# Transposing q and k on the way in instead of on TensorE, and making scores two batches ahead, in a fused sliding-window attention and GEGLU kernel

## The chip, the cores and the metric

The kernel runs on one core of a Trainium2 chip. The metric is the time of one execution in device microseconds. TensorE (PE in the profile) multiplies, VectorE (DVE) and ScalarE (ACT) do elementwise work, GpSimd (POOL) and SyncE (SP) only issue DMAs here.

## The reference

Attention over 8 batches, 8 heads, 576 positions, 64 channels per head, followed by a gated feed-forward layer on the 4608 resulting rows of 512:

```
scores = q @ k^T / 8
mask, heads 0..3 ("plain"):   0 <= i - j < 32
mask, heads 4..7 ("dilated"): 0 <= i - j < 128 and (i - j) % 4 == 0
attn = softmax(where(mask, scores, -1e9));  x = attn @ v      # per head
out  = (gelu(x @ w_gate) * (x @ w_val)) @ w_out               # 512 -> 1536 -> 512
```

A plain query sees at most 32 keys before it. A dilated query sees only keys of its own class (its position modulo 4), at most 32 of them, so each class of 144 positions is a plain window of its own.

## The kernel before

The work has two kinds. The unit of the attention is a "row tile" n: one batch and one pair of heads, so four per batch (two plain pairs, two dilated) and 32 in all. The unit of the feed-forward layer is a chunk c of 512 output rows, nine in all. A batch has 576 rows, so chunk c needs batches c and, but for its first rows, nothing later than c+1.

A row tile passes these steps. `t_q` and `t_k` transpose q and k on TensorE into PSUM (L152 and L170, `t_mm`), 18 transposes in all, the four classes of a 512-position block one by one and the 64 remaining positions apart; `copy` brings them to SBUF (ACT at L184, DVE at L186). `emit_s` makes the scores of four key blocks and a tail block with ten matmuls (L228) in PSUM banks 4 to 7, exponentiates them on ACT (L234, L235) and multiplies with a 0/1 mask on DVE (L236). `emit_pv` multiplies with v and with ones, for the row sums (L297). `norm_r` (L302 to L306) turns the sums into reciprocals along the free dimension on DVE and `norm_x` (L317 plain, L320 dilated) multiplies and writes the transposed result xT, which is FFN1's input. No maximum is subtracted.

A chunk has FFN1, 12 steps of 8 matmuls (L332) with gelu on ACT (L336) and the product on DVE (L337), and FFN2, four blocks of 12 matmuls (L341), each followed by a copy to SBUF (`osb`, L354 on DVE) and a store that SP issues (L356). Each matmul moves 512 columns.

Instructions run in program order on each engine; the schedule is written out by hand in the loop over chunks. A prologue makes all of batch 0. In chunk c the row tiles of `t_list` are transposed between FFN1's steps, those of `pv_list` get their PV and normalisation between FFN1's steps, and the scores of `s_list` are made between FFN2's blocks. When a score's batch is needed by the very next chunk (`now_pv`, chunks 0 and 1), PV and normalisation stand between FFN2's blocks as well, and FFN2 then uses one PSUM bank for all four blocks:

```
bank = 0 if now_pv else tb
ffn2(c, tb, bank)
do_s()
do_pv()
store(c, tb, bank)
```

Loads are issued by POOL in program order, fp32 in DRAM to fp16 in SBUF: q, k of batch 0, v of batch 0, gate and value weights, q, k of batch 1, output weights, v of batch 1, then in chunk c q, k and v of batch c+2. A q or k load (L117) has rows of four positions, 1 KB in DRAM; the plain half of v (L130) has rows of one position, 256 B.

Of the kernel before, what the change touches and what calls it, by code (L numbers as in the profile page):

```python
# [14 lines left out]
WIN = 32  # L15
# [24 lines left out]
def kernel(  # L40
# [22 lines left out]
    scale = 1.0 / np.sqrt(D)  # L63

# [10 lines left out]
    vpl = ctx.enter_context(tc.tile_pool(name="vpl", bufs=4))  # L75
    qtp = ctx.enter_context(tc.tile_pool(name="qtp", bufs=8))
# [18 lines left out]
    u_t = [const.tile([P, CH], F16, tag=f"u{i}", name=f"u{i}") for i in range(NNB)]  # L95

# [14 lines left out]
    tiles = {}  # L111
    def load_qk(b):
        qm = ldp.tile([P, H, 4, D], F16, tag="qm", name=f"qm{b}")
        km = ldp.tile([P, H, 4, D], F16, tag="km", name=f"km{b}")
        rem = ldp.tile([P, H, D], F16, tag="rem", name=f"rem{b}")
        for t, src in ((qm, q), (km, k)):
            nc.gpsimd.dma_start(  # L117
                out=t.rearrange("p h r d -> p h (r d)"),
                in_=src[b, :, 0 : 4 * P, :].rearrange("h (p r) d -> p h (r d)", r=4),
            )  # L120
        nc.gpsimd.dma_start(out=rem[0:64], in_=q[b, :, 4 * P : S, :].rearrange("h p d -> p h d"))
        nc.gpsimd.dma_start(out=rem[64:128], in_=k[b, :, 4 * P : S, :].rearrange("h p d -> p h d"))
        tiles["qk", b] = (qm, km, rem)

    def load_v(b):
        vp = vpl.tile([P, 4, 4, D], F16, tag="vp", name=f"vp{b}")
        vd = vpl.tile([P, 4, 4, D], F16, tag="vd", name=f"vd{b}")
        vt = vpl.tile([P, H, D], F16, tag="vt", name=f"vt{b}")
        for kb in range(4):
            nc.gpsimd.dma_start(  # L130
                out=vp[:, kb, :, :],
                in_=v[b, 0:4, kb * P : (kb + 1) * P, :].rearrange("h p d -> p h d"),
            )
        nc.gpsimd.dma_start(out=vt, in_=v[b, :, S - P : S, :].rearrange("h p d -> p h d"))
# [9 lines left out]

    def t_q(n, bank, eng_main, eng_rem):
        b, hp = divmod(n, NHP)
        qm, km, rem = tiles["qk", b]
        qk = qtp.tile([P, 2, S], F16, tag="qkT", name=f"qkT{n}")
        tiles["qkT", n] = qk
        t_mm(qm, hp, bank)  # L150
        for hl in range(2):
            nc.tensor.transpose(  # L152
                ps16[64 * hl : 64 * hl + 64, bank, 512:640], rem[:, 2 * hp + hl, :], ident
            )
        t_main(n, 0, bank, eng_main)
        src = ps16[:, bank, 512:640]
        if is_plain(n):
            copy(eng_rem, qk[:, :, 4 * P : S], src.rearrange("p (t u) -> p t u", t=2))
        else:
            copy(  # L160
                eng_rem,
                qk[:, 0, :].rearrange("p (r i) -> p r i", r=4)[:, :, P:NCL],
                src[:, 0:64].rearrange("p (i r) -> p r i", r=4),
            )
            copy(eng_rem, qk[:, 1, 4 * P : S], src[:, 64:128])

    def t_mm(src, hp, bank):
        for r in range(4):
            for hl in range(2):
                nc.tensor.transpose(  # L170
                    ps16[64 * hl : 64 * hl + 64, bank, r * P : (r + 1) * P],
                    src[:, 2 * hp + hl, r, :],
                    ident,
                )

    def t_k(n, bank, eng_main):
        b, hp = divmod(n, NHP)
        qm, km, rem = tiles["qk", b]
        t_mm(km, hp, bank)
        t_main(n, 1, bank, eng_main)  # L180
# [300 lines left out]
```

## Time and profile before

| | us |
|---|---|
| time, median of 3 runs (lowest to highest) | 450.51 (448.86 to 451.04) |
| the profiled execution | 451.33 |
| its span, first to last instruction | 449.5 |
| PE busy | 369.9 (82%) |
| DVE busy | 218.5 (49%) |
| ACT busy | 184.0 (41%) |
| POOL busy (issuing DMAs) | 69.1 (15%) |

Busy shares are averages over stages that differ, so they don't say what a stage waits for; the busy time by stage and the chain of waits do. Matmuls overlap, so the duration of one is longer than the step from one to the next. The granted clock of TensorE is given as a share of full speed.

### The profile page before, as it was taken

The page shows a single profiled execution, that of the slowest core. Times are in us where ns is not written, and L with a number is a line of the kernel's source. Part 1 is how long each engine was busy: PE and PEld are TensorE (multiplying, and loading weights), DVE is VectorE, ACT ScalarE, POOL GpSimd, SP SyncE. Part 2 cuts the span into 40 slices and gives each one's busy share as a digit, 9 for nine tenths or more (in the row PEclk, how much of TensorE's full clock was granted, in tenths as well). Part 3 has the DMA queues.
Part 4 walks back from the last instruction along what each step waited for, and adds up shares of the span by engine and source line. Part 5 has one row for each costly group of instructions (what it writes and reads, how often), then busy time and mean ns, then how long its engine had stood idle before and what let it go on. Part 6 is the DMA issues. An engine that isn't in the chain of part 4 may idle for free.

```text
span 449.5 us, 7001 instructions
## 1 busy us (share of the span) xinstructions
PE 369.9 (82%) x2960; PEld 177.7 (40%) x2960; DVE 218.5 (49%) x315; ACT 184.0 (41%) x288; POOL 69.1 (15%) x93
## 2 busy tenths in 40 slices
PE   0637975556777555799999999999999999999996
PEld 0523433222333222345445445544544444444442
DVE  0484314334211534678367656845774793332332
ACT  1531465120666411655647555654655220230320
POOL 6723606000052500000600510000000000000000
PEclk9955999668999988899999999999999999999999
DMA  9999969301069910000930591002001101101002
GB/s 164 181 204 200 180 50 137 53 23 47 1 79 96 155 45 25 25 1 4 149 108 2 73 139 48 1 1 95 0 3 48 48 0 48 47 1 70 23 2 94
DMA packets 64928, 30.03 MB, mean 67 GB/s; under 512 B 34944, under 2 KB 60032, under 8 KB 64896
## 3 DMA queue, kind: packets, MB, share of 16 engines
q0 software_dynamic: 59280, 19.40, 39.4%
q1 hardware_dynamic: 5616, 10.17, 6.0%
q8 instruction: 23, 0.38, 0.3%
q14 instruction: 9, 0.07, 0.0%
HBM read 39.53 MB, written 9.44 MB: 109 GB/s over the span
## 4 chain that ended last, share of the span: by engine, by line
PE 78%; DVE 12%; ACT 6%; DMA 2%; issue 1%; POOL 1%; DVEq 0%; POOLq 0%
PE ps L332 43%; PE ps L341 24%; PE ps L170 5%; PE ps L297 4%; ACT qkT L184 3%; PE ps L228 3%; DVE rb L306 2%; DVE xT L320 2%; DVE dt L302 2%; DMA rem<-in_k_dram 2%; DVE P L236 2%; ACT P L234 1%; DVE osb L354 1%; ACT P L235 1%; DVE xT L317 1%; DVE rc L304 1%
## 5 line engine op out<-in xcount | busy, mean ns | idle before, releaser
L341 PE MATMUL ps<-wo,u 128*128 128x512 f16 x432 | 108.6, 409 | 29.8 <-DVE osb L354 29.8
L337 DVE SCALAR_TENSOR_TENSOR u<-g,ps 128x512 f16<-128x512 f16 x108 | 74.3, 688 | 113.4 <-PE ps L332 106.1
L332 PE MATMUL ps<-xT,wg 128*128 128x512 f16 x432 | 114.3, 387 | 5.0 <-DVE xT L320 4.7
L336 ACT ACTIVATE g<-ps 128x512 f16<-128x512 f32 x108 | 65.7, 608 | 127.2 <-PE ps L332 125.0
L332 PE MATMUL ps<-xT,wv 128*128 128x512 f16 x432 | 112.7, 384 | 0.0
L184 ACT COPY qkT<-ps 128x512 f16<-128x512 f16 (+2 forms) x102 | 61.0, 668 | 48.8 <-PE ps L152 28.1
L341 PEld LDWEIGHTS <-u 128*128 128x128 f16 x432 | 43.3, 104 | 85.4 <-issue 43.3
L332 PEld LDWEIGHTS <-wv 128*128 128x128 f16 x432 | 42.8, 99 | 57.7 <-issue 5.6
L234 ACT ACTIVATE P<-ps 128x800 f16<-128x800 f32 (+1 forms) x32 | 25.7, 804 | 74.3 <-PE ps L228 74.2
L332 PEld LDWEIGHTS <-wg 128*128 128x128 f16 x432 | 38.4, 99 | 44.9 <-issue 3.0
L354 DVE TENSOR_SCALAR osb<-ps 128x512 f32<-128x512 f32 x36 | 24.5, 689 | 27.1 <-PE ps L341 27.1
L236 DVE TENSOR_TENSOR P<-P,mask_d 128x1296 f16<-128x1296 f16 x16 | 13.2, 831 | 38.7 <-ACT P L235 38.7
L117 POOL DMA_DIRECT2D qm<-in_q_dram x8 | 7.3, 909 | 154.8 <-PE ps L152 151.6
L236 DVE TENSOR_TENSOR P<-P,mask_p 128x1440 f16<-128x1440 f16 x16 | 14.5, 908 | 27.9 <-ACT P L235 27.9
L302 DVE STREAM_TRANSPOSE dt<-ps 128x576 f32<-128x576 f32 x32 | 25.0, 781 | 3.3 <-PE ps L297 3.3
L170 PE MATMUL ps<-ident,km 128*64 128x128 f16 x256 | 14.0, 232 | 14.4 <-ACT qkT L184 14.4
L306 DVE STREAM_TRANSPOSE rb<-rc 128x576 f32<-128x576 f32 x32 | 24.9, 778 | 1.1
L130 POOL DMA_DIRECT2D vp<-in_v_dram x32 | 24.1, 786 | 6.0 <-DMA km<-in_k_dram 2.0
L320 DVE TENSOR_TENSOR xT<-ps,rb 128x576 f16<-128x576 f32 x16 | 23.0, 1436 | 0.2
L235 ACT ACTIVATE P<-ps 128x640 f16<-128x640 f32 (+1 forms) x32 | 21.5, 672 | 0.0
L170 PE MATMUL ps<-ident,qm 128*64 128x128 f16 x256 | 14.2, 236 | 8.8 <-DMA qm<-in_q_dram 8.8
L228 PE MATMUL ps<-qkT 64*128 64x160 f16 (+3 forms) x320 | 17.2, 234 | 4.5 <-ACT P L234 1.9
(32 smaller groups left out, 194.2 us busy)
## 6 DMA issues: line engine op xcount, KB each, us to landing
out_dram<-osb SPq DMA_DIRECT2D x36, 256.0 KB, 2.0
qm<-in_q_dram POOLq DMA_DIRECT2D x8, 512.0 KB, 6.1
km<-in_k_dram POOLq DMA_DIRECT2D x8, 512.0 KB, 8.3
vp<-in_v_dram POOLq DMA_DIRECT2D x32, 64.0 KB, 6.9
vd<-in_v_dram POOLq DMA_DIRECT2D x8, 256.0 KB, 4.5
wg<-in_moe_w_gate_dram POOLq DMA_DIRECT2D x3, 512.0 KB, 10.7
wv<-in_moe_w_val_dram POOLq DMA_DIRECT2D x3, 512.0 KB, 12.4
wo<-in_moe_w_out_dram POOLq DMA_DIRECT2D x3, 512.0 KB, 16.2
```

Source lines behind the costliest of these rows:

```text
L170: nc.tensor.transpose(ps16[64 * hl : 64 * hl + 64, bank, r * P : (r + 1) * P], src[:, 2 * hp + hl, r, :], ident,)
L184: nc.scalar.copy(dst, src)
L228: nc.tensor.matmul(o, lhs, rhs, start=True, stop=True)
L234: nc.scalar.activation(pvh[:, :, 0:half], sb[:, 0, :, 0:half], AF.Exp, bias=0.0, scale=scale)
L236: nc.vector.tensor_tensor(pv, pv, mask_p if is_plain(n) else mask_d, ALU.mult)
L302: nc.vector.transpose(dt.rearrange("p b c -> p (b c)"), den)
L306: nc.vector.transpose(rb.rearrange("p (b c) -> p b c", c=32), bass.AP(tensor=rc.tensor, offset=rc.offset, ap=[rc.ap[0], [1, 18], [0, 32]]),)
L320: nc.vector.tensor_tensor(dst.rearrange("p (i b s) -> p b s i", b=2, s=2), num, rb.rearrange("p (b s i) -> p b s i", b=2, s=2), ALU.mult,)
L332: nc.tensor.matmul(ps[:, b0 + gi, :], w[:, kc, ns], xT[kc][:, tok], start=(kc == 0), stop=(kc == NKC - 1))
L336: nc.scalar.activation(g, ps[:, b0, :], AF.Gelu)
L337: nc.vector.scalar_tensor_tensor(u_t[nb], g, USCALE, ps[:, b0 + 1, :], ALU.mult, ALU.mult)
L341: nc.tensor.matmul(ps[:, bank, :], u_t[fc][:, tb * P : (tb + 1) * P], wo_t[fc // 4][:, fc % 4, :], start=(fc == 0), stop=(fc == NNB - 1),)
```

## The change

q and k of batches 1 to 7 are no longer transposed on TensorE. POOL loads them as before into SBUF, and SP then issues DMA transposes from SBUF to SBUF (`dma_start_transpose`), seven per batch. The plain heads are loaded in five blocks of 128 positions for that. Batch 0 is still transposed on TensorE, with the plain heads loaded first.

The transposed q and k of batch b are complete before its scores are made, and scores come a batch earlier: chunk 0 makes those of batches 1 and 2 (eight row tiles), chunk c those of batch c+2. Only chunk 0 has PV and normalisation in its tail. The first S of a chunk stands after FFN1's last step, the next ones inside FFN2's blocks: `ffn2` takes the number of the matmul before which they stand, and a function that makes them.

In dilated heads, two neighbouring classes (2m and 2m+1) of one head lie on the two halves of the 128 partitions after a transpose. A dilated row tile has 16 score matmuls (per head and class one of 144 columns and one of 16, the latter for the last 16 positions of a class) in place of ten, and one exponential in place of two. PV has 24 matmuls as before; `norm_x` writes in the order of positions.

The first batch's mask is added in PSUM: before the scores, four matmuls of the identity with a bias tile (0 or -60000, made from the mask on DVE) fill the banks. All other batches keep the multiplication on DVE, with one mask read for both heads or all four blocks. Stores are issued by ACT instead of SP. Buffers of v go from four to three, with a separate buffer for the last 16 positions per class that four memsets fill with zeros once. Output weights are loaded after v of batch 1.

```
     def load_qk(b):
+        qp = ldp.tile([P, 5, 2, HK, D], F16, tag="qp", name=f"qp{b}")
+        qd = ldp.tile([P, 2, HK, 4, D], F16, tag="qd", name=f"qd{b}")
+        rd = ldp.tile([16, 2, HK, 4, D], F16, tag="rd", name=f"rd{b}", bufs=1)
+        for t, src in ((0, q), (1, k)):
+            nc.gpsimd.dma_start(
+                out=qd[:, t].rearrange("p h r d -> p h (r d)"), in_=quads(src, b, HK, 0, 4 * P)
+            )
...
+        for kb in range(5):
+            n = min(P, S - kb * P)
+            for t, src in ((0, q), (1, k)):
+                nc.gpsimd.dma_start(
+                    out=qp[0:n, kb, t],
+                    in_=src[b, 0:HK, kb * P : kb * P + n, :].rearrange("h p d -> p h d"),
+                )
+        qtp_ = qtp.tile([P, 2, 2, S], F16, tag="qTp", name=f"qTp{b}")
+        qtd_ = qtp.tile([P, 2, HK, 2, NCL], F16, tag="qTd", name=f"qTd{b}")
+        tiles["qT", b] = (qtp_, qtd_)
+        dst = qtd_.rearrange("p t h m i -> p (t h m) i")
+        nc.sync.dma_start_transpose(out=dst[:, :, 0:P], in_=qd.rearrange("p t h r d -> p (t h r d)"))
+        nc.sync.dma_start_transpose(out=dst[:, :, P:NCL], in_=rd.rearrange("p t h r d -> p (t h r d)"))
+        dst = qtp_.rearrange("p t h c -> p (t h) c")
+        for kb in range(5):
+            n = min(P, S - kb * P)
+            nc.sync.dma_start_transpose(
+                out=dst[:, :, kb * P : kb * P + n], in_=qp[0:n, kb].rearrange("p t h d -> p (t h d)")
+            )
...
     def emit_s(n, b0, pe_mask=False):
...
+            if pe_mask:
+                for i in range(4):
+                    mm(ps[:, b0 + i, 0:DW], ident, bias_d, start=True, stop=False, skip_group_check=True)
+            for hl in range(2):
+                for m in range(2):
+                    for c0, k0, q0, q1 in ((m * NCL, 0, 0, NCL), (2 * NCL + 16 * m, 16, P, NCL)):
+                        for s in range(2):
+                            kt = qtd_[64 * s : 64 * s + 64, 1, 2 * hp + hl, m, :]
+                            qt = qtd_[64 * s : 64 * s + 64, 0, 2 * hp + hl, m, :]
+                            o = ps[:, b0 + 2 * s + hl, c0 : c0 + q1 - q0]
+                            mm(o, kt[:, k0 : k0 + P], qt[:, q0:q1], start=st, stop=True, skip_group_check=True)
...
     def norm_x(n, b0):
...
-            num = ps[:, b0 : b0 + 2, 0 : 2 * NCL].rearrange("p b (s i) -> p b s i", s=2)
+            num = ps[:, b0 : b0 + 2, 0 : 2 * NCL].rearrange("p s (m i) -> p i m s", m=2)
             nc.vector.tensor_tensor(
-                dst.rearrange("p (i b s) -> p b s i", b=2, s=2),
+                dst.rearrange("p (i m s) -> p i m s", m=2, s=2),
                 num,
-                rb.rearrange("p (b s i) -> p b s i", b=2, s=2),
+                rb.rearrange("p (s m i) -> p i m s", s=2, m=2),
                 ALU.mult,
             )
...
-        nc.sync.dma_start(out=out[t0 : t0 + P, :], in_=osb)
+        nc.scalar.dma_start(out=out[t0 : t0 + P, :], in_=osb)
...
     for c in range(NCH):
...
+        pv_list = list(range(NHP * (c + 1), NHP * (c + 2))) if 1 <= c < B - 1 else []
+        if c == 0:
+            s_list = list(range(NHP, 3 * NHP))
+        elif c + 2 < B:
+            s_list = list(range(NHP * (c + 2), NHP * (c + 3)))
+        else:
+            s_list = []
...
+            if nb == NNB - 1 and (c == 0 or c + 2 < B):
+                emit_s(emit_s_pe, SB)
...
+        if c == 0:
+            ffn2(c, 0, 0)
+            store(c, 0, 0, "dve")
+            ffn2(c, 1, 0, 3, s_next)
+            store(c, 1, 0, "dve")
+            pv_all(NHP, 1)
+            ffn2(c, 2, 0, 3, s_next)
+            store(c, 2, 0, "act")
+            pv_all(NHP + 1, 1)
+            ffn2(c, 3, 0, 3, s_next)
+            store(c, 3, 0, "act")
+            pv_all(NHP + 2, 1)
+            s_next()
+            pv_all(NHP + 3, 1)
+            while s_list:
+                s_next()
+        else:
+            ffn2(c, 0, 0)
+            store(c, 0, 0, "act")
+            ffn2(c, 1, 1, 5, s_next)
+            store(c, 1, 1, "act")
+            ffn2(c, 2, 2, 0, s_next)
+            ffn2(c, 3, 3, 0, s_next)
+            store(c, 2, 2, "act")
+            store(c, 3, 3, "dve")
```

## Rows read from the trace of the kernel before

**Rows 1.** The page's first line.

```profile
span 449.5 us, 7001 instructions
```

**Rows 2.** Busy time by stage; the first line names the columns.

```profile
core 0: us, PE busy (x) PEld busy (x) DVE busy (x) ACT busy (x) POOL busy (x), PEclk, DMA share, GB/s
0.00:38.93 38.93, 13.66 (x212) 10.48 (x213) 18.77 (x31) 11.45 (x14) 19.79 (x30) 0.80 1.33 184
38.93:70.14 31.21, 26.41 (x167) 11.81 (x168) 7.57 (x11) 15.22 (x27) 12.92 (x17) 0.92 1.14 126
70.14:110.68 40.54, 23.00 (x189) 10.37 (x188) 18.00 (x25) 7.84 (x10) 5.34 (x8) 0.75 0.50 69
110.68:147.86 37.18, 27.59 (x239) 13.28 (x240) 7.57 (x11) 23.07 (x41) 11.43 (x15) 1.00 0.60 62
147.86:188.62 40.76, 22.60 (x225) 11.07 (x226) 18.70 (x27) 11.10 (x16) 4.09 (x6) 0.86 0.43 55
188.62:217.12 28.50, 28.50 (x266) 13.70 (x267) 21.05 (x30) 17.27 (x30) 4.13 (x6) 0.96 0.20 30
229.53:256.80 27.27, 27.27 (x266) 13.30 (x266) 19.56 (x29) 15.02 (x27) 4.12 (x6) 1.00 0.23 42
256.80:269.22 12.42, 12.42 (x90) 5.63 (x90) 5.86 (x8) 7.86 (x10) 3.64 (x5) 1.00 1.25 145
348.61:373.26 24.65, 24.18 (x193) 11.82 (x192) 19.28 (x29) 7.16 (x12) 0.00 (x0) 1.00 0.06 22
383.62:414.70 31.08, 31.08 (x145) 14.07 (x144) 11.02 (x16) 7.16 (x12) 0.00 (x0) 1.00 0.09 34
```

**Rows 3.** Chain of waits, prologue and start of chunk 0: start us, us, what.

```profile
3.80 9.43 DMA rem<-in_k_dram
...
22.48 0.70 DVE dt L302
...
37.44 1.44 DVE xT L320
38.93 15.83 PE ps L332 x61
```

**Rows 4.** TensorE's waits: line, releaser, us in total, times, longest.

```profile
PE ps L341 <- DVE osb L354: 29.8, 6, 5.3
PE ps L170 <- ACT qkT L184: 14.4, 12, 1.5
```

**Rows 5.** Timeline of chunk 0's tail: start us, us, engine, line, operation.

```profile
72.69 0.91 DVE L236 TENSOR_TENSOR P<-P,mask_p 128x1440 f16<-128x1440 f16 x1 [1.75 <-ACT P L235]
...
78.60 0.68 DVE L354 TENSOR_SCALAR osb<-ps 128x512 f32<-128x512 f32 x1
...
79.34 5.28 PE L341 MATMUL ps<-wo,u 128*128 128x512 f16 x12 [4.85 <-DVE osb L354]
```

**Rows 6.** DMA queues (packets, MB, share); issues (count, KB, us to landing).

```profile
q0 software_dynamic: 59280, 19.40, 39.4%
q1 hardware_dynamic: 5616, 10.17, 6.0%
...
out_dram<-osb SPq DMA_DIRECT2D x36, 256.0 KB, 2.0
...
ident<-attn_identity SPq DMA_DIRECT2D x1, 32.0 KB, 1.9
```

**Rows 7.** Groups by line and shape: count, busy us, mean ns, idle before.

```profile
L130 POOL DMA_DIRECT2D vp<-in_v_dram x32 | 24.1, 786 | 6.0 <-DMA km<-in_k_dram 2.0 <-DMA qm<-in_q_dram 1.9 <-DMA wv<-in_moe_w_val_dram 1.8
L320 DVE TENSOR_TENSOR xT<-ps,rb 128x576 f16<-128x576 f32 x16 | 23.0, 1436 | 0.2
L236 DVE TENSOR_TENSOR P<-P,mask_p 128x1440 f16<-128x1440 f16 x16 | 14.5, 908 | 27.9 <-ACT P L235 27.9
...
L317 DVE TENSOR_TENSOR xT<-ps,rb 128x576 f16<-128x576 f32 x16 | 12.1, 753 | 0.2
```

**Rows 8.** The store's line: duration ns, min, median, max.

```profile
L356 SPq DMA_DIRECT2D out_dram<-osb x36: 332/332/373, 79.3 to 446.5; - x36
```

More of the change, by code (lines that the diff above doesn't have):

```diff
@@ L63 @@
     scale = 1.0 / np.sqrt(D)
+    PW, PT, DW = 160, 80, 320
+    POFF = [0, PW, 2 * PW + PT, 3 * PW + PT, 2 * PW]
+    PH = 4 * PW + PT
+    PB = 2 * PW + PT
     ctx.enter_context(tc.manual_schedule())
@@ L95 @@
     u_t = [const.tile([P, CH], F16, tag=f"u{i}", name=f"u{i}") for i in range(NNB)]
+    vr_t = [const.tile([P, HK, 4, D], F16, tag=f"vr{i}", name=f"vr{i}") for i in range(3)]
+    rem0 = const.tile([P, HK, 4, D], F16, tag="rem0")
+    nc.vector.memset(rem0, 0.0)
+    for t in vr_t:
+        nc.vector.memset(t, 0.0)
     ps = psum.tile([P, 8, 512], F32, tag="ps")
@@ L131, in load_v @@
                 out=vp[:, kb, :, :],
-                in_=v[b, 0:4, kb * P : (kb + 1) * P, :].rearrange("h p d -> p h d"),
+                in_=v[b, 0:HK, kb * P : (kb + 1) * P, :].rearrange("h p d -> p h d"),
             )
-        nc.gpsimd.dma_start(out=vt, in_=v[b, :, S - P : S, :].rearrange("h p d -> p h d"))
+        nc.gpsimd.dma_start(out=vt, in_=v[b, 0:HK, S - P : S, :].rearrange("h p d -> p h d"))
+        nc.gpsimd.dma_start(out=vd.rearrange("p h r d -> p h (r d)"), in_=quads(v, b, HK, 0, 4 * P))
         nc.gpsimd.dma_start(
-            out=vd.rearrange("p h r d -> p h (r d)"),
-            in_=v[b, 4:8, 0 : 4 * P, :].rearrange("h (p r) d -> p h (r d)", r=4),
+            out=vr[P - 16 : P].rearrange("p h r d -> p h (r d)"), in_=quads(v, b, HK, 4 * P, S)
         )
-        tiles["v", b] = (vp, vd, vt)
+        tiles["v", b] = (vp, vd, vt, vr)
     def is_plain(n):
         return n % NHP < NHP // 2
[L145 to L180, printed above, removed]
     def copy(eng, dst, src):
@@ L186, in copy @@
             nc.vector.tensor_copy(dst, src)
-    def t_main(n, t, bank, eng):
-        qk = tiles["qkT", n]
-        src = ps16[:, bank, 0:512].rearrange("p (r i) -> p r i", r=4)
-        if is_plain(n):
-            dst = qk[:, t, 0 : 4 * P].rearrange("p (i r) -> p r i", r=4)
-        elif t == 0:
-            dst = qk[:, t, :].rearrange("p (r i) -> p r i", r=4)[:, :, 0:P]
-        else:
-            dst = qk[:, t, 0 : 4 * P].rearrange("p (r i) -> p r i", r=4)
-        copy(eng, dst, src)
-    def geom(n):
-        mw, tw = (160, 80) if is_plain(n) else (144, 72)
-        off = [0, mw, 2 * mw + tw, 3 * mw + tw, 2 * mw]
-        return mw, tw, off, 4 * mw + tw
@@ L238, in emit_pv, with out_ap @@
     def emit_pv(n, b0):
-        b, hp = divmod(n, NHP)
-        vp, vd, vt = tiles["v", b]
+        b, hp = n // NHP, n % 2
+        vp, vd, vt, vr = tiles["v", b]
         pt = tiles.pop(("P", n))
-        o = [ps[:, b0 + i, :] for i in range(3)]
-        mw, tw, off, hw = geom(n)
+        def out_ap(hl, bank, c0, dims):
+            base = ps[64 * hl : 64 * hl + 64, b0 + bank, c0 : c0 + 1]
+            return bass.AP(tensor=base.tensor, offset=base.offset, ap=[base.ap[0]] + dims)
+        mms = []
@@ L244, in emit_pv @@
         if is_plain(n):
-            mms = [
+            for bank, c0, c1, j, pc, den, st in (
                 (0, 0, 160, 0, 0, False, True),
@@ L299, in norm_r @@
+        for o, lhs, rhs, st in mms:
+            nc.tensor.matmul(o, lhs, rhs, start=st, stop=True, skip_group_check=True)
     def norm_r(n, b0):
@@ L347, in ffn2, with store @@
             )
-    def store(c, tb, bank, eng="dve"):
+    def store(c, tb, bank, eng):
         osb = osbp.tile([P, DM], F32, tag="osb")
```

342 lines of the change are left out of this document (194 added, 148 removed).

## The prediction

> **What bounds the kernel now.** I read the page first, then the busy time by stage, then the chain of waits, and last the timeline of the stages in which TensorE isn't busy.
>
> The profiled execution has a span of 449.5 us and took 451.33 us, so 1.8 us lie around the span; the median of the three runs is 450.51 us, 0.8 below it [rows 1]. I sum against the profiled execution.
>
> The stages [rows 2] are: prologue (first batch's attention) 38.93 us; then for each 512-token chunk c a first part (FFN1, with transposes and PV between its matmuls) and a tail (FFN2, with the scores of a later batch). The reader is to compare like stages. FFN1 of chunk c takes 31.21, 37.18, 28.50 and 27.27 us for c = 0, 1, 2 and 3 (c = 4 and 5 are like 3), 24.65 us for c = 6, which has PV but no transposes. A tail takes 12.42 us for c = 3, but 40.54 and 40.76 for c = 0 and 1. Chunk 7 has FFN alone: 31.08 us for 144 matmuls, 0.216 each, TensorE never idle. So TensorE is the bound from 188.6 us on, and the two tails of 40 us are a chain through three engines.
>
> In those tails the scores of the batch that the very next chunk needs are made, exponentiated, masked, multiplied with v and normalised, and FFN2 has one bank: the copy that frees it stands on DVE behind a whole normalisation. The timeline shows it: mask at 72.69, the copy to osb not before 78.60, and the next FFN2 matmuls after 4.85 us of idle TensorE [rows 5]. Six such waits make 29.8 us of idle TensorE; transposes waiting for their bank's copy make another 14.4 [rows 4]. The granted clock is 0.75 and 0.86 of full in the tails, 1.00 in steady chunks [rows 2]; after that 4.85 us idle, 12 matmuls take 5.28 us, 0.44 each, which is the lower level (1.2 GHz) against 0.216 at 2.4.
>
> **The change part by part.**
>
> *PE transposes of batches 1 to 7 go* (504 of them and their copies out of PSUM). Chunk 6 shows FFN1 with four PV and without transposes: 24.65 us. Chunks 3, 4, 5: 27.27 to 24.65, three times 2.6 = 7.9 us. Chunk 2: 28.50 to 24.65, 3.9. Chunk 1 has all 24.65 of PV and FFN1 after the change, against 37.18 with eight transposed tiles: 12.5. Chunk 0 has FFN1 alone. Its first 61 matmuls took 15.83 us, partly at the lower clock [rows 3]; the other 35 at 0.216 give 7.6, so 23.4 against 31.21: 7.8 us. ACT copies vanish off the path.
>
> *Scores two batches ahead.* Chunk 1 then has no PV in its tail: four S between FFN2 blocks, as chunk 3 has, 12.42 against 40.76: 28.3 us, the largest term. The S now stand inside FFN2 blocks; an S costs (12.42 - 48 x 0.216) / 4 = 0.5 us of TensorE either way. Dilated S has 16 matmuls instead of 10, eight of them 16 columns wide; between no more and 0.5 us more per tile, 7 us over 14 tiles: I take 0, the pairs' columns being fewer.
>
> *Tail of chunk 0.* It still has PV of batch 1, and S of batches 1 and 2, eight in place of four. DVE was busy 18.00 us there [rows 2]. After: four more masks at 0.9 [rows 7], two osb copies of 0.68 [rows 5] fewer (they go to ACT), 18.0 + 3.6 - 1.4 = 20.2 us, and the first mask comes 2.6 us in, as now [rows 2, 5]. FFN2's bank is freed before the normalisation, not behind it, since store and PV are reordered; blocks 2 and 3 are freed by ACT. TensorE has 48 x 0.216 + 8 x 0.5 + 4 x 0.8 (PV, a quarter of 24.65 - 20.7 less a wait) = 17.6 us, which lies beside DVE at full clock. That gives 23 us of DVE chain and about 25 with the last S waiting for each other's exponentials. At the lower clock TensorE alone needs 35, and with waits 39. I take 28, near the full clock, since the gaps shrink from nearly 5 us to under 3. 40.54 to 28: 12.5 us.
>
> *Prologue.* Transposes begin when q, k of 8 heads have landed, a DMA wait of 9.43 us that ends at 13.2; then the chain of four normalisations begins at 22.48 and ends at 38.88 [rows 3]. Half the heads come first now, so the wait should end some 4 us sooner; masks leave DVE for four matmuls a tile with an identity, beside the DVE chain. Against that: two bias tiles and four memsets on DVE ahead of the rest, on the bias of which the first S wait, and a POOL load that waits for one memset. Bounds: 1 us lost to 7 won; I take 4 won.
>
> *Row tiles by class parity.* The dilated normalisation took 1.44 us where the plain one takes 0.75 [rows 7]; its new order writes contiguously but reads across two banks. Bounds 0.75 to 2.9 (twice as now); taken at 1.44. In the steady chunks it is hidden by 20.7 us of FFN1; its price where cover is gone is two per prologue and chunk-0 tail, so -2.8 to +5.8 us.
>
> *Stores to ACT's queue.* Thirty-six issues of 0.33 us [rows 8], 1.3 us a chunk on ACT, and in each chunk ACT waits for one osb from DVE before its next gelu. ACT has 7.2 us of work in 24.65 [rows 2], and two spare PSUM banks cover a gelu that is 2 us late. 0, up to 1 us in each of 9 chunks.
>
> *Loads.* Plain q and k come in rows of 256 B rather than 1 KB: per batch 2 x (4 x 128 + 4 x 16 + 4 x 576) = 5760 packets, and v 4 x (512 + 128 + 128 + 16) = 3136, together 8896 against 6656. A software packet took 0.394 x 16 x 449.5 us / 59280 = 48 ns of one engine [rows 6], so about 26.7 us of all 16, beside a chunk of 37. They overlapped to a share of 1.33 in the prologue [rows 2]: 20 us. POOL issues 21 per batch at 0.79 us [rows 7], 16.5 us: hidden too.
>
> *The crossbar DMAs.* Nothing in this trace transposes by DMA. A batch has 36 blocks of 128 x 128 fp16 (16 dilated, 2 for its 16-row rest, 18 plain), 1.18 MB. Lower bound: the pace of a store, 256 KB landing in 2.0 us, 9.2 us a batch. Upper: each block as long as the identity's 32 KB load, 1.9 us, one after another, 68 us a batch [rows 6]. Between: 4608 pieces of 256 B at 48 ns, 13.8 us. I take 9 to 14, nearer the store, the only row here of a large DMA out of SBUF that SP issues: its issue takes SP 0.33 us [rows 8], not the landing's 2.0, so several can be under way. SP has nothing else queued now; behind a late transpose stand only later transposes, and TensorE waits for them in the S of that batch, with FFN2 behind.
>
> The Trainium skill, "DMA: Bandwidth & Descriptors", section "Latency and other measured facts", gives 261 GB/s for such transposes, which would be 4.5 us a batch and take away the 2 us allowed below. Its page "VectorE: DVE Perf Modes", section "The three transpose paths", gives 1309 ns for one 128 x 128 block, which, if blocks went one by one, would be 47 us a batch and 25 + 329 + 113.3 + 1.8 = 469 us in all, by the rival's sum below. No row of this trace decides between them.
>
> *Is it in time?* Up to the transposed q, k of batch 1: 2688 (batch 0) + 3136 (v) + 3072 (gate and value weights) + 5760 packets = 14656 x 48 ns / 16 = 44, plus 13.8, over 1.33, plus 2 us start = 45 us; needed when FFN1 of chunk 0 ends, 35 + 23.4 = 58. The output weights, now behind v of batch 1: 19328 packets, 58 + 13.8, over 1.33, plus 2 = 56, needed at 59. Batch 2: 25 thousand packets, 75 + 27.6, over 1.33, plus 2 = 79; its first S stands behind all four FFN2 blocks, four S and three PV, some 16 us into the tail, at 74. So 0 to 5 us late: I add 2. Later batches have a chunk of 37 us each.
>
> **Sum.** 7.9 + 3.9 + 12.5 + 7.8 + 28.3 + 12.5 + 4 = 76.9; 449.5 - 76.9 + 2 = 374.6; with 1.8 around the span, 376 us.
>
> **Rivals.**
> - *The clock stays low in chunk 0's tail* and TensorE's 35 us bound it: 39 instead of 28, plus a slow start of chunk 1: 376 + 14 = 390. For it: 0.75 granted there now. Against: shorter gaps.
> - *Transposes late, not slow throughout*: they can begin when the dilated half of batch 1 has landed (10048 packets, 30 over 1.33, plus 2 = 25 us). At 35 us a batch, batch 1 is ready at 60, 2 late, batch 2 at 95, another 18, and later ones hide behind chunks of 37: 396. At 40 us it is 7, 23 and some 15 over the rest: 421. I put it at 405, with 392 to 448 around it. For it: the loads fill the 16 engines in just that stretch (share 1.33 and 1.14, [rows 2]). Against: it takes more than twice the 13.8 us.
> - *Transposes one by one, slower than before.* At T us a batch the seventh is ready at 25 + 7T; then come chunk 5's tail (12.4) and all from chunk 6 on (449.5 - 348.6 = 100.9). It equals 449.5 at T = 44.5 us, 1.24 us a block; from there on the change loses. At 50 it gives 488 + 1.8 = 490 us, at 68 616 us; I put it at 490. For it: the identity's 1.9 us. Against: that is one DMA's latency, while stores of eight times the size land in 2.0.
> - *The change doesn't do what it says*: S of batch 2 in chunk 0 pushes PV of batch 1 back so that chunk 0 gives up what chunk 1 wins. PV of batch 1 stands ahead of three of those four S on TensorE, so I give this nothing of its own beyond the first rival.
>
> **How the numbers follow.** Forecast (366 to 386) 0.52; clock low in the tail (386 to 400) 0.17; late transposes (392 to 448) 0.15; one by one (over 453) 0.10; below 366, with the prologue and normalisation at their good ends, 0.04; within 0.5% of now 0.02. About 0.5% (2.3 us) is what a measurement here tells from no change. Faster 0.88, same 0.02, slower 0.10. Range 364 to 425: it leaves out the slow case, the top third of the late one, the 0.02 and half of the case below.
>
> **What would show it.** Right: no transposing matmuls after the prologue; tails of chunks 1 to 5 near 12.4 us at clock 1.00; FFN1 of chunks 1 to 5 near 24.7; the tail of chunk 0 at 25 to 30 with no osb wait over 2 us; no S matmul waiting for a transpose DMA. Wrong: S waiting for qTp or qTd in every chunk (one by one) or in chunk 0 alone (late); a tail of chunk 0 near 40 at a clock under 0.8; an osb wait on ACT that delays gelu until TensorE idles.

## The result, and the profile after

The changed kernel takes 375.05 us (median of four runs, 374.63 to 376.37) against 450.5 (four runs, 448.86 to 451.04) on the same chip: a ratio of 0.8335, with an interval of 0.8305 to 0.8366. The forecast was 376. The profiled execution took 374.63 us, its span is 372.9 us. First the head of its page; the columns are busy time, share of the span and number of instructions:

```profile
span 372.9 us, 6286 instructions
...
PE 341.8 (92%) x2556; PEld 164.5 (44%) x2556; DVE 196.6 (53%) x285; ACT 144.4 (39%) x204; POOL 120.2 (32%) x175
...
PEclk9996799977999999999999999999999999999999
DMA  9999999999999999989417101100110020011002
...
q0 software_dynamic: 75440, 19.15, 55.1%
q1 hardware_dynamic: 32576, 8.56, 16.2%
```

TensorE is busy 92% of the time and at 90% of the full clock or more from the eleventh slice on. The DMA engines are what has filled up: they are busy 90% or more in each of the first 17 slices, some 158 us. The transposes are queue q1's; 16.2% of 372.9 us over seven batches is 8.6 us of all 16 engines for one batch (a little less, since three small loads share that queue). Software packets (q0) took 0.551 x 16 x 372.9 / 75440 = 43.6 ns, against 48 before.

The busy time by stage, in the columns of [rows 2]. The lines are: prologue; FFN1 and tail of chunk 0; the same of chunk 1; the same of chunk 2; then FFN1 of chunk 6 and the whole of chunk 7.

```profile
0.00:37.09 37.09, 17.06 (x227) 11.40 (x228) 17.16 (x27) 12.62 (x16) 23.04 (x37) 0.92 1.29 169
37.09:59.31 22.22, 22.22 (x93) 9.43 (x92) 7.57 (x11) 7.30 (x13) 15.20 (x22) 0.91 1.54 187
59.31:85.40 26.09, 19.71 (x249) 10.94 (x248) 18.33 (x26) 11.78 (x14) 18.87 (x28) 0.87 1.68 187
85.40:111.83 26.43, 26.27 (x198) 12.24 (x196) 19.41 (x29) 9.90 (x15) 21.03 (x32) 0.93 1.80 159
111.83:124.35 12.52, 12.52 (x102) 5.83 (x102) 4.16 (x5) 8.10 (x10) 11.06 (x16) 1.00 1.75 186
124.35:148.80 24.45, 24.29 (x194) 11.70 (x194) 18.81 (x28) 8.55 (x14) 15.23 (x23) 1.00 1.53 146
148.80:161.31 12.51, 12.51 (x101) 5.84 (x102) 4.16 (x5) 8.09 (x10) 2.53 (x4) 1.00 0.96 143
272.21:296.66 24.45, 24.29 (x194) 11.83 (x192) 18.81 (x28) 8.34 (x13) 0.00 (x0) 1.00 0.06 22
307.02:338.10 31.08, 31.08 (x146) 14.07 (x144) 8.96 (x13) 8.97 (x15) 0.00 (x0) 1.00 0.09 35
```

Read it line against line with [rows 2]. Chunk 1's tail is now a tail like any other (12.52 us, 40.76 before). From chunk 2 on, FFN1 takes 24.45 us with four PV in it, whether loads and transposes run beside it (DMA share 1.53) or not (0.06). Between the prologue and the last stores only chunk 0's tail still has TensorE idle for long, 26.09 - 19.71 = 6.4 us, at a clock of 0.87.

Where the 76.6 us of span went, stage by stage (us; forecast terms beside):

| stage | before | after | won | forecast |
|---|---|---|---|---|
| prologue | 38.93 | 37.09 | 1.8 | 4 |
| FFN1, chunk 0 | 31.21 | 22.22 | 9.0 | 7.8 |
| tail, chunk 0 | 40.54 | 26.09 | 14.5 | 12.5, less 2 for late transposes |
| FFN1, chunk 1 | 37.18 | 26.43 | 10.8 | 12.5 |
| tail, chunk 1 | 40.76 | 12.52 | 28.2 | 28.3 |
| FFN1, chunk 2 | 28.50 | 24.45 | 4.1 | 3.9 |
| FFN1, chunks 3 to 5 | 3 x 27.27 | 3 x 24.45 | 8.5 | 7.9 |
| the rest | | | -0.2 | 0 |

TensorE's longer waits after, in the columns of [rows 4]:

```profile
PE ps L221 <- DMA qm_first<-in_q_dram: 7.2, 1, 7.2
PE ps L393 <- DVE xT L416: 4.4, 8, 3.1
...
PE ps L293 <- DMA qTp<-qp: 2.3, 1, 2.3
...
PE ps L444 <- DVE osb L457: 1.2, 2, 1.0
```

The two groups that stood in [rows 4] with 29.8 and 14.4 us are gone: FFN2 waits 1.2 us in all for its bank, and nothing transposes on TensorE after the prologue. In all seven batches TensorE waits once for a transpose DMA, 2.3 us.

### The profile page after: what moved, and what is told of

Its sections match the earlier page's. It is cut to its first block, busy times and chain, and to the rows that moved or that the text cites. A ratio compares the mean times of both kernels' runs of the same rounds, so it can differ in the third digit from the quotient of the medians.

```text
span 372.9 us, 6286 instructions
## 1 busy us (share of the span) xinstructions
PE 341.8 (92%) x2556; PEld 164.5 (44%) x2556; DVE 196.6 (53%) x285; ACT 144.4 (39%) x204; POOL 120.2 (32%) x175
## 3 DMA queue, kind: packets, MB, share of 16 engines
q0 software_dynamic: 75440, 19.15, 55.1%
q1 hardware_dynamic: 32576, 8.56, 16.2%
## 4 chain that ended last, share of the span: by engine, by line
PE 83%; DVE 11%; ACT 2%; DMA 2%; issue 1%; POOL 0%; DVEq 0%; POOLq 0%
PE ps L433 46%; PE ps L444 25%; PE ps L393 7%; DVE xT L416 3%; DVE dt L398 2%; DVE rb L402 2%; PE ps L310 2%; PE ps L293 2%; DMA qm_first<-in_k_dram 2%; DVE u L438 1%; ACT P L296 1%; DVE rc L400 1%; DVE qTp L208 1%; PE ps L282 1%; DVE osb L457 1%
## 5 line engine op out<-in xcount | busy, mean ns | idle before, releaser
L444 PE MATMUL ps<-wo,u 128*128 128x512 f16 x432 | 98.4, 380 | 1.2 <-DVE osb L457 1.2
L444 PEld LDWEIGHTS <-u 128*128 128x128 f16 x432 | 40.2, 98 | 48.7 <-issue 1.5
L166 POOL DMA_DIRECT2D qp<-in_q_dram x35 | 25.7, 735 | 14.4 <-DMA wg<-in_moe_w_gate_dram 4.1
L166 POOL DMA_DIRECT2D qp<-in_k_dram x35 | 25.8, 736 | 13.9 <-DMA qd<-in_k_dram 4.3
L312 ACT ACTIVATE P<-ps 128x1280 f16<-128x1280 f32 x16 | 19.8, 1237 | 17.7 <-PE ps L310 15.6
L455 ACT ACTIVATE osb<-ps 128x512 f32<-128x512 f32 x26 | 15.5, 597 | 26.2 <-PE ps L444 26.2
L457 DVE TENSOR_SCALAR osb<-ps 128x512 f32<-128x512 f32 x10 | 6.9, 690 | 31.8 <-PE ps L444 31.8
L317 DVE TENSOR_TENSOR P<-P,mask_d 128x1280 f16<-128x1280 f16 x14 | 11.5, 824 | 17.6 <-ACT P L312 17.6
L296 ACT ACTIVATE P<-ps 128x800 f16<-128x800 f32 x16 | 13.4, 837 | 14.6 <-PE ps L293 14.5
L393 PE MATMUL ps<-P,ones 128*64 128x64 f16 (+4 forms) x320 | 15.7, 228 | 0.0
L393 PE MATMUL ps<-P,vd 128*64 128x144 f16 x128 | 8.7, 242 | 6.1 <-DVE xT L416 4.4
```

The lines of the kernel that those rows point to most:

```text
L166: nc.gpsimd.dma_start(out=qp[0:n, kb, t], in_=src[b, 0:HK, kb * P : kb * P + n, :].rearrange("h p d -> p h d"),)
L312: nc.scalar.activation(pt, ps[:, b0 : b0 + 4, 0:DW], AF.Exp, bias=0.0, scale=scale)
L317: nc.vector.tensor_tensor(pt, pt, mb, ALU.mult)
L393: nc.tensor.matmul(o, lhs, rhs, start=st, stop=True, skip_group_check=True)
L444: nc.tensor.matmul(ps[:, bank, :], u_t[fc][:, tb * P : (tb + 1) * P], wo_t[fc // 4][:, fc % 4, :], start=(fc == 0), stop=(fc == NNB - 1),)
```

## The experiments

Twelve kernels ran, each beside the kernel before on the same chip. The theory was that the gain is the sum of three separate things: transposes off TensorE, scores two batches ahead, and a shorter chain in chunk 0's tail, with the DMA transposes hidden. The rivals were that the transposes set the time, or that one part does nearly all.

**Scores two batches ahead, alone** (kernel before, transposes still on TensorE).

```
-        t_stop = need if c == 0 else min(NU, NHP * (c + 3))
+        t_stop = min(NU, NHP * (c + 3))
```

> The kernel before, with one line changed: chunk 0 transposes (on TensorE) and scores batch 2 as well as batch 1. Theory (scores two batches ahead are worth a chunk-1 tail by themselves): chunk 1 falls from 78 us to 41 (FFN1 28.5, tail 12.4), chunk 0 pays for four more transposed tiles (FFN1 31.2 to 37) and four more scores in its tail (40.5 to 47): 451 - 37 + 12.5 = 426 us. Rival (only the crossbar makes it pay, since the transposes and scores merely move into chunk 0): chunk 0 gives back what chunk 1 wins, 445 to 452 us.

434.15 us, ratio 0.9625 (0.9584 to 0.9666). FFN1 of chunk 0, its tail, and the whole of chunk 1, in the columns of [rows 2]:

```profile
37.82:89.60 51.78, 38.11 (x239) 17.25 (x240) 7.57 (x11) 24.49 (x41) 22.53 (x30) 0.70 1.11 119
89.60:131.30 41.70, 23.50 (x224) 11.23 (x225) 18.70 (x27) 10.35 (x16) 3.74 (x5) 0.82 0.41 53
131.30:172.34 41.04, 41.04 (x353) 19.32 (x353) 26.93 (x38) 25.14 (x39) 7.75 (x10) 0.97 0.51 65
```

Chunk 1 falls as said, from 77.94 us [rows 2] to 41.04. But chunk 0's FFN1 now transposes two batches, all of them in four of its twelve steps, and grows from 31.21 to 51.78 us (37 were expected), of which TensorE is idle 13.7, at a clock of 0.70. With the transposes so placed, being two ahead costs more than half of what it wins; the third experiment places them better.

**The copy ahead of PV, alone** (kernel before).

```
             do_s()
-            do_pv()
             store(c, tb, bank)
+            do_pv()
```

> The kernel before, with one thing changed: in FFN2's tails the copy that frees FFN2's bank (osb) stands before PV and normalisation instead of behind them. Theory (the copy queued behind the normalisation on DVE is what makes the two tails 40 us): each tail falls to about 26 us, the DVE work in it, 451 - 28 = 423 us, and the waits of FFN2 for osb fall from 29.8 us to under 8. Rival (the tails are bound by the chain score, exponential, mask, PV, normalise itself): tails stay over 36 us, 443 us or more.

431.0 us (428.09 and 433.91), ratio 0.9555 (0.9471 to 0.964). FFN2's waits, which were 29.8 us in [rows 4]:

```profile
PE ps L341 <- DVE osb L354: 13.0, 6, 2.3
```

The longest falls from 5.3 to 2.3 us, and one moved line gives about 20 us (16.8 and 22.6 in the two runs). It was expected to give 28, with waits under 8 us in all: the six waits shrink but do not vanish, each still ending with the copy on DVE. In the profiled run, the faster one, the two tails take 27.2 and 29.2 us, where 26 were expected.

**Both together, without the crossbar** (kernel before; chunk 0's transposes begin at step 3 instead of 7).

```
-        t_stop = need if c == 0 else min(NU, NHP * (c + 3))
+        t_stop = min(NU, NHP * (c + 3))
...
-            first = 7 if c == 0 else 2
+            first = 3 if c == 0 else 2
...
             do_s()
-            do_pv()
             store(c, tb, bank)
+            do_pv()
```

> The kernel before with both schedule edits and no crossbar: batch 2 transposed on TensorE and scored in chunk 0 (its transposes spread over eight FFN1 steps), and the osb copy ahead of PV and normalisation. Theory (the rest of the gain is TensorE's transposes): chunk 0's FFN1 37 us, its tail 29, chunk 1 30.5 + 12.4, the later chunks as before: 451 - 11.5 - 6.8 - 28.4 + 6.3 = 411 us, so the crossbar with its prologue would be worth 35 us of the 75. Rival (schedule alone does it): under 390 us.

411.35 us, ratio 0.9142 (0.9073 to 0.9211), as expected. Chunk 0's FFN1 takes 40.0 us in its trace, 12 less than with the transposes crowded into four steps. Of the 75 us, 39 come from order alone; the other 36 from the rest of the change. Half of these lie in chunk 0's FFN1 (40.0 to 22.2 us), which then holds no transposes; no kernel puts the transposes alone back on TensorE and keeps all else.

**The old order back in chunk 0's tail** (changed kernel).

```
-            ffn2(c, 0, 0)
-            store(c, 0, 0, "dve")
-            ffn2(c, 1, 0, 3, s_next)
...
+            for tb in range(4):
+                ffn2(c, tb, 0)
+                s_next()
+                pv_all(NHP + tb, 1)
+                store(c, tb, 0, "dve")
```

> The changed kernel with chunk 0's tail in the old order (score, PV, normalise, then the osb copy on DVE; all else as changed). Theory (order sets the tail): the tail of chunk 0 goes from 26 to about 43 us, with TensorE waits on osb of 13 to 15 us: 375 + 17 = 392 us. Rival (the tail is bound by DVE work and by the crossbar's transposes, in either order): 375 to 380 us.

393.37 us, ratio 0.8721 (0.8676 to 0.8767): 18 us lost, and the wait of [rows 5] is back with its old length:

```profile
PE ps L444 <- DVE osb L457: 14.5, 3, 5.0
```

The tail takes 45.4 us in this trace against 26.09. So chunk 0's short tail is the order's doing, not that of faster inputs. The order has three parts that this edit takes back together: the copy ahead of PV, two of the four copies on ACT, and the scores inside FFN2's blocks.

**Scores one batch ahead again** (changed kernel; batches 2 and 3 are scored in chunk 1's tail, with batch 2's PV there).

```
-        pv_list = list(range(NHP * (c + 1), NHP * (c + 2))) if 1 <= c < B - 1 else []
+        pv_list = list(range(NHP * (c + 1), NHP * (c + 2))) if 2 <= c < B - 1 else []
         if c == 0:
-            s_list = list(range(NHP, 3 * NHP))
+            s_list = list(range(NHP, 2 * NHP))
+        elif c == 1:
+            s_list = list(range(2 * NHP, 4 * NHP))
...
-        if c == 0:
+        if c < 2:
...
```

> The changed kernel without the second batch in chunk 0: batch 2 is scored in chunk 1's tail together with batch 3, and its PV and normalisation stand there too, in the new order of chunk 0's tail. Theory (with crossbar transposes and the new order a tail with PV costs 26 us, not 41, so two batches ahead is worth much less than the 28 us that the prediction put on it): chunk 0's tail 26 to 23, chunk 1 from 39 to 48: 375 + 6 = 381 us. Rival (two batches ahead is the largest term whatever the tail looks like): 375 + 25 = 400 us or more.

385.85 us, ratio 0.8555 (0.8514 to 0.8597): 10.8 us lost. Chunk 1 takes 48.7 instead of 39 us, and chunk 2 starts at a low clock (its first 16 matmuls take 5.87 us instead of 3.45). The expected loss was 6 us; the slow start, which makes chunk 2 2.3 us longer, was not in it. The stage table books 28 us under this edit; with the better order in both tails, being two ahead is worth 11. A term read off a stage is a price in one order of subtraction, and the parts here overlap.

**No transposes at all** (changed kernel; SP issues none, the scores of batches 1 to 7 read two tiles of zeros instead, so transposing is left out).

```
-        nc.sync.dma_start_transpose(out=dst[:, :, 0:P], in_=qd.rearrange("p t h r d -> p (t h r d)"))
...
+        tiles["qT", b] = (qtp_c, qtd_c)
```

> The changed kernel without the DMA transposes: scores of batches 1 to 7 read two constant tiles of zeros, all loads stay, so what is left out is the transposes and every wait on them. Theory (they are hidden: the one wait for them, 2.3 us of TensorE before a score of batch 2, lies beside a normalisation on DVE that ends later): 374 to 376 us, no more than 1 us gained. Rival (that wait, and the transposes' share of the 16 DMA engines, is on the path): 371 to 372 us.

375.11 us, ratio 0.8335 (0.8294 to 0.8377): the same as with them. FFN1 and tail of chunk 0 and FFN1 of chunk 1:

```profile
38.40:60.60 22.20, 22.20 (x93) 9.49 (x92) 7.56 (x11) 7.22 (x13) 15.19 (x23) 0.90 1.31 145
60.60:86.86 26.26, 19.72 (x250) 11.03 (x250) 18.65 (x26) 11.86 (x14) 24.02 (x36) 0.87 1.40 140
86.86:113.00 26.14, 25.97 (x193) 12.11 (x192) 19.16 (x29) 9.67 (x14) 22.99 (x35) 0.93 1.39 120
```

The DMA share falls from 1.54 and 1.68 to 1.31 and 1.40, and the stages stay. The 2.3 us for which TensorE waits at the transposes of batch 2 therefore cost nothing: the tail is the DVE chain, as reckoned. (Two added memsets of 1.02 us each stand on this kernel's chain; its prologue is 1.3 us longer.)

**Every transpose three times, to the same place** (changed kernel).

```
-        nc.sync.dma_start_transpose(out=dst[:, :, 0:P], in_=qd.rearrange("p t h r d -> p (t h r d)"))
+        for _ in range(3):
+            nc.sync.dma_start_transpose(out=dst[:, :, 0:P], in_=qd.rearrange("p t h r d -> p (t h r d)"))
...
```

> The changed kernel with every DMA transpose issued three times, to the same place. One batch took 17 us from the first issue to the last landing (11 us of it issuing); three times is 38 to 42 us. Theory (the reckoning of the prediction, with start at 35 us: a batch's transposes must fit a chunk of 37 us, with some 7 us of slack for batch 1 and none for batch 2): batch 1 is 14 to 16 us late, batch 2 another 19 to 21, batch 3 another 6 to 8, the rest 1 to 3 each: 415 to 435 us. Rival 1 (still hidden): under 385. Rival 2 (transposes and loads slow each other on the 16 engines): over 450.

572.14 us, ratio 1.2716 (1.2629 to 1.2802): far above the theory and on the rival's side, but for a reason that neither named. It stands in SP's waits and, in the second fence, in the times from issue to landing (count, median us):

```profile
SPq L182 <- DMA qTp<-qp: 138.6, 70, 5.4
```

```profile
qTp<-qp SPq DMA_TRANSPOSE x105, 2.5
qTd<-qd SPq DMA_TRANSPOSE x21, 4.6
qTd<-rd SPq DMA_TRANSPOSE x21, 2.9
```

A repeat writes where the one before it writes, so the program makes it wait on that one's completion semaphore: 70 waits, two for each of 35. This run therefore does not measure three times the load but one DMA at a time, 3 x (5 x 2.5 + 4.6 + 2.9) = 60 us a batch. That is the third rival made real, and its sum holds: batch 1 starts at 36, 36 + 7 x 60 + 113 for all that follows is 569 us, and the span is 570.4. It also prices that rival: issued one after another and once each, a batch takes 20 us, well under a chunk's 37. Those 36 blocks of 128 x 128 are 0.56 us each on average. The Trainium skill, "VectorE: DVE Perf Modes", section "The three transpose paths", gives 1309 ns for a block; the DMAs of four blocks and of sixteen came out at 0.63 and 0.29 us a block here.

**Every transpose twice, the second into a tile that nobody reads** (changed kernel).

```
+        nc.sync.dma_start_transpose(out=dum[:, :, 0:P], in_=qd.rearrange("p t h r d -> p (t h r d)"))
+        nc.sync.dma_start_transpose(out=dum[:, :, P:NCL], in_=rd.rearrange("p t h r d -> p (t h r d)"))
...
```

> The changed kernel with every DMA transpose issued twice, the second time to a buffer that nobody reads, so that the two need not wait for each other. Theory (SP issues a batch's seven in 11 us and the pace is set by issuing; batch 1 has 7 us of slack, batch 2 none): issuing 23 us a batch, batch 1 ready at about 63 (4 us late), batch 2 at 88 to 91, 6 to 8 us late after a normalisation that hides the first 3; later batches hidden in 37 us: 385 to 388 us. Rival 1 (the slack is larger, all hidden): under 378. Rival 2 (the 16 DMA engines are full in that stretch and loads come later too): over 395.

412.41 us, ratio 0.9164 (0.9116 to 0.9211): 37 us lost, where the theory allowed 10 to 13. The second rival's bound held. The theory reckoned 23 us of SP's time for a batch's fourteen issues; those of batch 1 took 31 (35.80 to 67.04), and the first exponential of batch 1 comes at 72.13 instead of 60.47. Then comes a second loss. Timeline of chunk 0's tail (start us, us, engine, line, operation, idle before and releaser):

```profile
77.36 0.69 DVE L466 TENSOR_SCALAR osb<-ps 128x512 f32<-128x512 f32 x1 [2.85 <-PE ps L453]
...
89.70 0.84 ACT L305 ACTIVATE P<-ps 128x800 f16<-128x800 f32 x1 [16.14 <-DMA qTp<-qp]
...
92.72 1.01 PE L453 MATMUL ps<-wo,u 128*128 128x512 f16 x2 [10.59 <-DVE osb L466]
```

The chain of waits in the same stretch (start us, us, what):

```profile
83.20 6.00 DMA qTp<-qp
...
89.28 0.38 ACTq L468
```

osb is ready at 78.05, but ACT issues its store only at 89.28. Behind it on ACT waits the exponential of the next scores, behind that their mask and the next copy on DVE, and behind that FFN2: TensorE idles 10.6 us. The chain says what holds the store: a transpose of q and k that was issued at 83.20 and lands at 89.20. In the trace's semaphore events both DMAs signal their landing on the same semaphore, and the store's issue waits for that semaphore first. So it is the program that ties a store to a transpose, in that both share a completion semaphore; osb itself has nothing to do with that transpose. Chunk 0 ends 26 us later than in the changed kernel; the other 10 us are lost in chunks 1 and 2, none from chunk 3 on. How much of the 31 us of issuing comes from engines that loads and transposes fill together was not isolated.

**Stores issued by SP again** (changed kernel).

```
-        nc.scalar.dma_start(out=out[t0 : t0 + P, :], in_=osb)
+        nc.sync.dma_start(out=out[t0 : t0 + P, :], in_=osb)
```

> The changed kernel with its stores issued by SP again, behind the DMA transposes, instead of by ACT. Theory (the prediction's 0 for the move: SP's transposes wait at most for the scores of an earlier chunk, four osb buffers cover the delay, and ACT's issues were hidden): 374 to 377 us. Rival (a store stands behind transposes that wait for loads, its osb isn't freed, and FFN2 stalls): 380 us or more. Rival 2 (ACT's wait for an osb from DVE before its gelu did cost time): 372 us or less.

373.84 us (374 to 377 were expected), ratio 0.8315 (0.828 to 0.835): the same as the changed kernel, within error. At the present load of transposes it does not matter who issues the stores.

**First mask on DVE** (changed kernel).

```
-    emit_s(0, SB, pe_mask=True)
+    emit_s(0, SB)
...
-        emit_s(i, SB, pe_mask=True)
+        emit_s(i, SB)
```

> The changed kernel with the first batch masked on DVE as all others, instead of by four identity matmuls a row tile on TensorE. Theory (at the lower clock the identity matmuls of the first two tiles take 1.31 and 1.20 us on the chain to the first normalisation, a DVE mask 0.91 once): prologue 1 us shorter, 374 us. Rival (DVE is the prologue's bound, so four masks of 0.9 are added to it): 377 to 379 us.

377.56 us, ratio 0.8395 (0.835 to 0.8441); the expected 374 fell, and the rival's 377 to 379 held in its number but only in part in its reason: the prologue is 0.9 us longer, not 2 to 4. The chain of waits (start us, us, what) shows the rest at the end of chunk 0:

```profile
72.82 8.43 DMA qTp<-qp
81.29 0.51 PE ps L293 x6
```

In the changed kernel that same score step starts at 78.39 and leaves 0.3 us of idle TensorE before the PV behind it, which waits for the normalisation beside it. Here the loads of batch 2 come 1.5 us later and its transposes land 2.9 us later, and now they are on the chain. This shows how near the edge the transposes of batch 2 are; why the loads come later by more than the prologue was not isolated, and the intervals of the two kernels overlap.

**Old element order in the dilated normalisation** (changed kernel).

```
-            num = ps[:, b0 : b0 + 2, 0 : 2 * NCL].rearrange("p s (m i) -> p i m s", m=2)
+            num = ps[:, b0 : b0 + 2, 0 : 2 * NCL].rearrange("p s (m i) -> p s m i", m=2)
...
-                dst.rearrange("p (i m s) -> p i m s", m=2, s=2),
+                dst.rearrange("p (i m s) -> p s m i", m=2, s=2),
...
```

> The changed kernel with the old order of elements in the dilated normalisation (class by class, writing every fourth position) instead of the order of positions. Theory (the new order is worth 1.44 - 1.12 = 0.3 us wherever DVE is the chain: two tiles in the prologue, two in chunk 0's tail, and the fourth PV of six chunks): 375 + 1.2 + 1.9 = 378 us. Rival (hidden in the steady chunks): 376 us.

376.67 us (376.61 to 376.9), ratio 0.8371 (0.834 to 0.8402). 1.6 us lost, between the expected 378 and the rival's 376. The operation takes 1.44 us again, 1.12 in the changed kernel. The traces show where it counts: FFN1 of chunk 2 takes 24.76 us instead of 24.45, its chain running through the normalisation of the fourth PV, so each steady chunk loses 0.3 us. By the start of chunk 2 only 0.4 us are lost; with five steady chunks that makes the 1.9 us between the two spans (374.8 and 372.9). The ratios' intervals overlap, so the size is not certain.

**PV further apart in the steady chunks** (changed kernel).

```
-            if nb in (1, 3, 5, 7) and pv_list:
+            if nb in (1, 3, 6, 9) and pv_list:
```

> The changed kernel with the four PV of a chunk behind FFN1's steps 1, 3, 6 and 9 instead of 1, 3, 5 and 7. Theory (in every FFN1 of chunks 1 to 6 the fourth PV waits for a dilated normalisation on DVE, 0.5 to 0.7 us of idle TensorE, because FFN1 without transposes leaves two steps too little time for it): FFN1 24.45 to 23.9 us in six chunks, 375 - 3 = 372 us. Rival (the stall is taken up elsewhere, for example by FFN1's steps that wait for u behind the later normalisation): 375 us.

374.96 us, ratio 0.8331 (0.8305 to 0.8356): no change; the expected 372 fell, the rival's 375 held. TensorE's waits for xT do get rarer, two instead of eight:

```profile
PE ps L393 <- DVE xT L416: 4.1, 2, 3.1
```

but the 4.4 us become only 4.1, of which one wait in the prologue is 3.1. There was nothing to win: TensorE is busy 24.29 of 24.45 us in those stages.

## Why the prediction was right

The mechanism held: the stages that were to shrink shrank, each for the reason given. The sum of 374.6 came within 1.7 us of the span of 372.9; that is in part luck, for single terms were off by more, in both directions: the prologue 2.2 and chunk 1's FFN1 1.7 too much, chunk 0 3.2 too little, and 2 were added for late transposes that were not paid. One sign of being right did not come: a score did wait for a transpose, once, for 2.3 us.

*Transposes off TensorE.* Right, and a little better than said (24.45 instead of 24.65 us per FFN1 with PV, 22.22 instead of 23.4 in chunk 0). The forecast held that FFN1 hides the dilated normalisation in the steady chunks; the run with the old element order shows that the fourth one isn't hidden, and that its new order is worth 0.3 us a chunk there. In chunk 1's FFN1 the term was 1.7 us too large: I took a stage at full clock, but this one starts after a tail with idle TensorE. The chain of waits of the changed kernel shows the same 16 matmuls at the start of chunk 1 and of chunk 2:

```profile
85.49 5.34 PE ps L433 x16
...
124.35 3.45 PE ps L433 x16
```

*Scores two ahead.* 28.3 us said, 28.2 measured, and the extra matmuls of a dilated score cost nothing visible, as taken. But it is 28 only when it is taken away first: the experiments give 16.6 alone and 10.8 last. The forecast's sum was safe because it compared complete stages of one kernel with complete stages of the other.

*Tail of chunk 0.* 28 said, 26.09 measured. DVE does 18.33 us there (20.2 said) and the first mask comes 2.6 us in. The timeline of that tail shows the new order at work:

```profile
61.93 0.91 DVE L317 TENSOR_TENSOR P<-P,mask_p 128x1440 f16<-128x1440 f16 x1 [1.75 <-ACT P L297]
...
62.76 0.68 DVE L457 TENSOR_SCALAR osb<-ps 128x512 f32<-128x512 f32 x1
...
63.49 0.81 PE L444 MATMUL ps<-wo,u 128*128 128x512 f16 x3 [1.00 <-DVE osb L457]
...
77.84 1.12 DVE L416 TENSOR_TENSOR xT<-ps,rb 128x576 f16<-128x576 f32 x1
78.39 0.35 PE L293 MATMUL ps<-qTp 64*128 64x80 f16 x6 [2.28 <-DMA qTp<-qp]
78.42 0.34 ACTq L459 DMA_DIRECT2D out_dram<-osb  x1
...
79.01 0.45 PE L393 MATMUL ps<-P,vd 128*64 128x144 f16 x4 [0.28 <-DVE xT L416]
```

The copy follows the mask directly, where in [rows 5] it came 5.9 us after it, and FFN2 goes on after 1.00 us. At the end a transpose releases TensorE at 78.39, but the next PV has to wait for the xT that ends at 78.96 anyway. (The store at 78.42 waits for the same transpose, by a shared semaphore as in the run with twice the transposes; its osb was ready at 75.72.) So the 2 us that I added for late transposes were not paid, and the first rival (a clock that stays low, 39 us) did not come: the granted clock was 0.87, and TensorE's longest gap there 2.3 us, against 4.85 in [rows 5].

*Prologue.* 4 us said, 1.8 measured: the mis-sized term. The wait for q and k ends at 8.53 instead of 13.23 [rows 3], 4.7 us earlier, as said. (The forecast had all transposes begin then; those of q begin earlier, at 8.81 before and at 7.20 after.) The chain of waits shows what took the rest:

```profile
2.12 6.41 DMA qm_first<-in_k_dram
...
9.26 1.30 DVE qTp L208
...
11.81 1.30 DVE qTp L208
...
13.47 1.31 PE ps L282 x4
...
19.66 1.20 PE ps L282 x4
...
22.16 0.79 DVE dt L398
```

From the end of that wait to the first normalisation the chain takes 13.6 us, where it took 9.3 before. Two sets of mask matmuls stand on it, 2.5 us, which I had put beside the DVE chain; the DVE mask of 0.9 us that they replace stood there before. Transposing takes 5.2 us of the chain instead of 2.4, and the copies of the transposed blocks (L208) 3.5 instead of 2.7. The first normalisation starts at 22.16 instead of 22.48. The other 1.5 us are in the main two dilated normalisations shorter by 0.3 each, and PV's matmuls: two pieces of 0.84 and 0.86 us on this chain, where the chain before has 1.43 and 1.35.

*Crossbar DMAs.* 9 to 14 us of all engines a batch were said, 8.6 measured. The Trainium skill, "DMA: Bandwidth & Descriptors", section "Latency and other measured facts", gives 261 GB/s, by which I estimated 4.5 us; the trace shows nearly twice that. The step that failed is a different one: SP's issue was taken at a store's 0.33 us [rows 8]. The times of the first two batches:

```profile
35.17 3.28 SPq L174 DMA_TRANSPOSE qTd<-qd  x1
38.55 1.16 SPq L175 DMA_TRANSPOSE qTd<-rd  x1
39.80 6.45 SPq L179 DMA_TRANSPOSE qTp<-qp  x5
59.81 3.27 SPq L174 DMA_TRANSPOSE qTd<-qd  x1
...
65.15 6.72 SPq L179 DMA_TRANSPOSE qTp<-qp  x5
```

Seven issues keep SP 11 to 12 us. With a median of 5.8 us from issue to landing, batch 1 is there at about 52 (45 said, needed at 59.3) and batch 2 at 78.4 (79 said). That the time agrees for batch 2 is a coincidence of two errors, packets faster than reckoned (43.6 ns) and a slower issue; the shares were not isolated. It cost no time, as the run without transposes shows. (A slip in the lower bound: 1.18 MB at the store's pace are 9.0 us, not 9.2.)

*Late transposes and the slow rival.* Late transposes did not come, but the margin is small: batch 2 was 0.3 us from the chain, and doubling the transposes cost 37 us. The one-by-one rival's formula was right and its price wrong: not 1.24 to 1.9 us a block but 0.56.

*Stores, loads.* Nothing to see in the time, as said: TensorE is busy 24.29 of 24.45 us in the steady chunks, stores and load issues beside it.

## What to carry to other kernels

When an operation moves to another engine, first ask which order it makes possible: here 39 of 75 us were to be had from order alone, one moved line giving 20, and the transposes on the crossbar then took 18 us out of the stage in which two-ahead scoring is paid for. Sum such a change by complete stages, and don't quote one part's share without saying what else is in place. A transfer that is hidden has a margin: find it by doubling the transfer, since here taking it away changed no time and doubling it took back half of the gain. And when a DMA is issued long after its data is ready, read in the chain of waits what released it: it may be the landing of another DMA that shares its semaphore.

## What the runs showed of the hardware that was not expected

- A DMA transpose takes SP 1.2 to 3.4 us to issue, not 0.33 as a store does; one at a time, in the run with three of each, it lands after 2.5 us (four blocks of 128 x 128) to 4.6 us (sixteen), in the changed kernel, with several under way beside loads, after 5.8 and 7.5.
- Waits at a DMA's issue can be the program's and not the hardware's: transposes to the same place waited at SP for one another's landing, 70 times in the run with three of each, and a store that ACT issues stood 11 us after its data was ready, until a transpose with the same completion semaphore had landed.
- With twice the transposes, single issues on SP took up to 5.7 us in the first 80 us, against 3.4 at most in the changed kernel. The Trainium skill, "DMA: Bandwidth & Descriptors", section "Rules for kernel authors", says that spreading DMAs over issuing engines saves only issue time, as all share the same 16 engines; with the stores back on SP the time is indeed the same.
